# Table phases of a state-space convolution: made by TensorE from fp16 parts instead of by VectorE

## The chip, the cores and the metric

The kernel runs on one core of one Trainium2 chip. The metric is the device time of one execution in microseconds (us); a ratio is the time after over the time before. The engines are called PE (TensorE, matrix products into PSUM), DVE (VectorE), ACT (ScalarE), POOL (GpSimd) and SP (SyncE, which issues most DMAs).

## What is computed

A residual block over 2048 positions and 512 channels: a long convolution whose kernel is a sum over 128 complex exponentials, and then a channel MLP.

```python
dt = exp(log_dt)[:, None]                       # (512, 1)
P  = exp(dt*(A_re + 1j*A_im)[:, :, None] * l)   # l = 0..2047, rounded to bf16
K  = einsum("dn,dnl,dn->dl", C, P, dt*B).real   # (512, 2048), a sum over n = 128
y  = irfft(rfft(pad(u)) * rfft(pad(K)))[:L] + u*Dskip
h  = x + y                       # u = layernorm(x)
out = h + W2.gelu(W1.layernorm(layernorm(h)) + b1) + b2
```

The step that the change is about is K. Position l is split as l = 8k + rest, so that each exponential is a product of two small tables: a B table over k (33 entries, -16 to 16, of which entry 0 is one) and an A table over the other part (20 entries, the list LA). Every entry is 128 rows (n) by 512 channels, complex: exp(real part) times cosine and sine of a phase. The phase of a B entry is 8k*psi, that of an A entry LA*psi plus the angle gamma of C*B*dt; psi is dt*A_im in units of 1/65536 of a turn, so that the low 16 bits of an integer are the phase and wrap by themselves.

## The kernel before

**Order.** Every operation is added to a list with a priority, a cost and what it reads and writes. A list scheduler (class Sched) then sets one fixed order per engine before the kernel runs: it takes what can start first by its costs, and by priority where several can. PSUM is handed out by the same planner as four slots of 128x1024 f32 (ps0 to ps3). On the chip each engine works through its list in order and waits where something isn't ready. SBUF is one tile, `ar`, cut up by address, so most rows of the profile read `ar<-ar` or `ar<-ps`.

**Stages, in the order of the program.**
- Constants: DFT tables T, TP1, TP2, BD, DD, W from integer codes on DVE and sines on ACT (lines 400 to 575; L441 is the helper for ACT activations, L422, L424, L429 and L434 are helpers for DVE operations).
- Parameters: six inputs are transposed by PE (L587), and `th` = dt*A_re, `psi` = dt*A_im, the size G of the coefficient C*B*dt and its angle `gam` are made, all 128x512 f32.
- Exponentials: 32 ACT instructions for the B table (L597) and 20 for the A table (L600), each 128x512 from `th` with a scale. Ten DVE products (L786) multiply the A table by G.
- Layernorm statistics of x (L673), normalised u (L693, L695), block DFT by PE (L697), its results copied out of PSUM (L358 on ACT, L360 on DVE) and sent to DRAM and back (AU_d); then the transform of x (xspec, L715).
- Tables, in two halves of 256 channels (`tables(0)`, `tables(1)`). Each half has nine groups of four entries: four B groups and five A groups. For a group DVE makes 4 code pieces of 128x256 (L422 or L434) and a second copy a quarter turn on (L422, 128x1024); ACT takes Sin of the low 16 bits of all 2048 codes in one instruction (L441); DVE multiplies the exponentials by sine and cosine (L773, L774 and a sign change L772 for a B group, which makes entries k and -k; L787, L788 for an A group). Code buffers and sine buffers are three deep. The imaginary tables of both halves lie in the same place, so `tables(1)` cannot write before kgen has read `tables(0)`.
- kgen(c), for channel blocks c = 0 to 3 of 128: 256 small matmuls (L807, L808) in four column tiles of PE; 0 and 1 need the first half, 2 and 3 the second.
- kspec(b,c), inverse(b,c): the kernel's transform and the inverse one (L846, L858, L882, L888), each with a trip through DRAM (AK_d, Z_d) to change layout; b = 0 and 1 are the two halves of the output positions.
- tail and mlp: residual, statistics (L968), the MLP (L1007, L1024), the output. tail(b) needs all four channel blocks of inverse(b).

SP's queue holds all DMAs of these trips, in one order; a DMA that waits holds up all behind it.

Of the kernel before, what the change touches and what calls it, by code (L numbers as in the profile page):

```python
# [14 lines left out]
i16 = mybir.dt.int16  # L15
P = 128
# [4 lines left out]
CW = 128  # L21
NCH = 4
# [75 lines left out]
SZ = {f32: 4, bf16: 2, i32: 4, i16: 2}  # L98
# [31 lines left out]
class Sched:  # L130
# [10 lines left out]
    def add(self, eng, cost, fn, r=(), w=(), new=(), lat=0.0, pr=None, byts=0):  # L141
# [4 lines left out]
        o.pr = self.pr if pr is None else pr  # L146
        deps = set()
# [23 lines left out]
    def run(self, nslots):  # L171
# [83 lines left out]
def kernel(ctx, tc, A_u, A_A_re, A_A_im, A_B_re, A_B_im, A_C_re, A_C_im, A_log_dt, A_Dskip,  # L255
# [43 lines left out]
    tiny = take(f32, 1)  # L299
# [100 lines left out]
    S.pr = 1  # L400
    table("trig_and_small")
# [45 lines left out]

    def ident_fn():
# [6 lines left out]
    POOL(0.3, lambda: gp.iota(i1.ap(), pattern=[[1, 32]], base=0, channel_multiplier=0), w=[i1])  # L455
    i4 = ct(i32, 16)
# [57 lines left out]
    valD = ct(f32, 2, 16)  # L514
    AC(valD, codD, ACT.Sin, scale=SINSC, oap=lambda: valD.ap().rearrange("p a b -> p (a b)"), iap=lambda: low16(codD), tbl=True)
# [31 lines left out]
    valW = ct(bf16, 4, 32)  # L547
    AC(valW, codW, ACT.Sin, scale=SINSC, oap=lambda: valW.ap().rearrange("p a b -> p (a b)"), iap=lambda: low16(codW), tbl=True)
    for v in range(7):
        for g in range(4):  # L550
            TS(W[v], valW, msk[4 * v + g:4 * v + g + 1], None, ALU.mult, n=128, mode=4, oap=lambda v=v, g=g: W[v].ap()[:, :, 32 * g:32 * g + 32])
    pm = take(f32, 1) if False else ct(f32, 1)
# [3 lines left out]

    for f0 in range(0, 16, 4):
        for half, TPx in ((0, TP1), (1, TP2)):
            p = Ps()

            def fn(e, f0=f0, half=half, p=p):
                o = pst(p)
                idp = identb.ap().rearrange("p (a s r) -> p s a r", a=4, r=2)
                for k in range(4):
                    for r in range(2):
                        pe.matmul(o[64 * r:64 * r + 64, 128 * k:128 * k + 128], lhsT=T.ap()[:, f0 + k, half, :], rhs=idp, start=True, stop=True, tile_position=(0, 64 * r))  # L566
            add("PE", 0.9, fn, r=[T, identb], w=[p], new=[p], pr=3)
            oap = lambda f0=f0, TPx=TPx: TPx[f0:f0 + 4].ap().rearrange("p a b -> p (a b)")
            if half == 0:
                add("ACT", c_act(512, 1), lambda e, p=p, oap=oap: act.activation(oap(), pst(p)[:, 0:512], ACT.Copy, scale=pm.ap()), r=[p, pm], w=[TPx[f0:f0 + 4]], pr=3)  # L570
            else:
                evac(oap, lambda p=p: pst(p)[:, 0:512], 512, [p], [TPx[f0:f0 + 4]], pr=3)

    S.pr = 2
# [21 lines left out]
    for a in range(NA):  # L599
# [507 lines left out]
```

## Time and profile before

| | us |
|---|---|
| runs of the kernel (3) | 374.4, 375.73, 375.84; median 375.73 |
| span of the profiled execution, from its first to its last instruction | 373.3 |
| DVE busy in the span | 217.9 |
| PE busy in the span | 207.6 |
| ACT busy in the span | 195.5 |

The page gives no other time for the profiled execution than its span; the runs lie 1.1 to 2.5 us above it, and the median 2.4. The granted clock of PE is told from 103 us on; before that the page shows 1.00 for want of a record, and the pace of the matmuls tells the level. Read first which engine is full in which stretch (the 40 slices), then how each stage ends.

### The profile page before, as it was taken

To read this page: it belongs to the slowest core of one execution; us is meant where nothing else is said; L and a number is where in the kernel's file an instruction comes from. 1 tells how busy PE (TensorE), PEld (TensorE's weight loads), DVE (VectorE), ACT (ScalarE), POOL (GpSimd) and SP (SyncE) were. 2 spreads that over 40 slices of the span, in tenths; PEclk is the share of its full clock that TensorE was granted. 3 is DMA by queue.
4 is the path that set the end of the run, shared out by engine and by line. 5 is a ranking of instruction groups with operands and counts; after the bars stand their busy time and mean duration, and the time that the engine had idled before them with its cause. 6 is when DMAs were issued, how large, how long until landed. Compare 5 with 4: busy or idle time off the path is not lost.

```text
span 373.3 us, 6724 instructions
## 1 busy us (share of the span) xinstructions
PE 207.6 (56%) x2697; PEld 130.3 (35%) x2712; DVE 217.9 (58%) x524; ACT 195.5 (52%) x240; POOL 6.6 (2%) x72
## 2 busy tenths in 40 slices
PE   1012206637004632154654773669959998699994
PEld 1001102116004521154433672126737652344441
DVE  8999999969999399900113650495443604920202
ACT  1259899998448263820523475447624553473340
POOL 5000000000000000000000000000000000000000
PEclk9999999999656965558855595769978999989999
DMA  7300000899900223793667796400796531010101
GB/s 204 122 0 0 1 0 15 213 207 235 218 14 3 71 68 112 152 217 98 191 145 211 213 276 153 105 1 2 209 256 146 150 87 28 3 29 14 44 15 42
DMA packets 70946, 39.84 MB, mean 107 GB/s; under 512 B 56097, under 2 KB 65794, under 8 KB 70914
## 3 DMA queue, kind: packets, MB, share of 16 engines
q1 hardware_dynamic: 69186, 38.88, 41.5%
q10 hardware_dynamic: 1728, 0.52, 0.8%
q8 instruction: 21, 0.34, 0.4%
q14 instruction: 11, 0.09, 0.1%
HBM read 20.52 MB, written 14.68 MB: 94 GB/s over the span
## 4 chain that ended last, share of the span: by engine, by line
PE 36%; DVE 30%; DMA 15%; ACT 7%; issue 7%; SPq 3%; DVEq 0%; ACTq 0%
PE ps L1007 10%; PE ps L1024 9%; DMA ar<-AU_d 5%; DVE ar L434 4%; DMA AK_d<-ar 4%; DMA Z_d<-ar 4%; DVE ar L429 4%; ACT ar L358 3%; DVE ar L422 3%; SPq L370 3%; PE ps L888 3%; PE ps L807 3%; DVE ar L673 3%; PE ps L697 3%; PE ps L808 3%
## 5 line engine op out<-in xcount | busy, mean ns | idle before, releaser
L358 ACT CAST ar<-ps 128x1024 bf16<-128x1024 f32 (+2 forms) x86 | 73.7, 898 | 88.1 <-PE ps L808 22.9
L441 ACT ACTIVATE ar<-ar 128x2048 bf16<-128x2048 int16 (+5 forms) x30 | 41.9, 1415 | 38.4 <-DVE ar L422 18.6
L1007 PE MATMUL ps<-ar 128*128 128x512 bf16 (+1 forms) x170 | 42.8, 401 | 1.7 <-ACT ar L358 1.3
L876 DVE TENSOR_TENSOR ar<-ar 128x1024 bf16<-128x1024 bf16 x48 | 30.2, 685 | 22.2 <-PE ps L888 15.7
L1024 PE MATMUL ps<-ar 128*128 128x512 bf16 (+1 forms) x169 | 41.4, 390 | 1.4 <-DVE ar L1026 0.8
L1009 ACT ACTIVATE ar<-ps,ar 128x512 bf16<-128x512 f32 (+1 forms) x44 | 30.2, 688 | 22.0 <-PE ps L1007 12.8
L360 DVE CAST ar<-ps 128x1024 bf16<-128x1024 f32 (+1 forms) x22 | 24.2, 1121 | 28.7 <-DMA AK_d<-ar 16.2
L1026 DVE TENSOR_TENSOR ar<-ps,ar 128x512 bf16<-128x512 f32 x16 | 10.9, 688 | 46.4 <-PE ps L1024 35.9
L807 PE MATMUL ps<-ar 128*20 128x33 bf16 x512 | 18.9, 250 | 30.8 <-DVE ar L788 24.0
L807 PEld LDWEIGHTS <-ar 128*20 128x20 bf16 x512 | 17.4, 124 | 40.4 <-DVE ar L788 26.0
L422 DVE TENSOR_SCALAR ar<-ar 128x256 int32<-128x256 f32 (+8 forms) x103 | 28.8, 327 | 0.9
L1007 PEld LDWEIGHTS <-ar 128*128 128x128 bf16 (+1 forms) x176 | 18.3, 105 | 22.7 <-issue 5.8
L1024 PEld LDWEIGHTS <-ar 128*128 128x128 bf16 (+1 forms) x176 | 17.2, 100 | 20.4 <-issue 2.6
L808 PE MATMUL ps<-ar 128*20 128x33 bf16 x512 | 18.9, 249 | 9.0 <-issue 9.0
L715 PE MATMUL ps<-ar 128*128 128x128 bf16 x128 | 13.5, 285 | 18.2 <-DMA ar<-AU_d 11.5
L434 DVE SCALAR_TENSOR_TENSOR ar<-ar 128x256 int32<-128x256 f32 (+4 forms) x77 | 22.2, 321 | 1.6 <-ACT ar L441 0.5
L858 PE MATMUL ps<-ar 128*128 128x128 bf16 x128 | 11.4, 254 | 20.6 <-DMA ar<-AK_d 12.7
L846 PE MATMUL ps<-ar 20*128 20x256 bf16 (+1 forms) x448 | 18.3, 321 | 6.6 <-ACT ar L358 6.5
L968 DVE BATCH_NORM_STATS2 ar<-ps 128x6 f32<-128x512 f32 x16 | 10.4, 688 | 19.3 <-PE ps L963 14.8
L566 PE MATMUL ps<-ar 128*64 128x128 bf16 x64 | 5.0, 291 | 27.8 <-ACT ar L570 13.1
L715 PEld LDWEIGHTS <-ar 128*128 128x128 bf16 x128 | 11.5, 132 | 21.2 <-DMA ar<-AU_d 13.6
L597 ACT ACTIVATE ar<-ar 128x512 bf16<-128x512 f32 x32 | 16.7, 613 | 3.5 <-DVE ar L429 3.5
(65 smaller groups left out, 292.9 us busy)
## 6 DMA issues: line engine op xcount, KB each, us to landing
AU_d<-ar SPq DMA_DIRECT2D x16, 256.0 KB, 3.8
ar<-AU_d SPq DMA_DIRECT2D x8, 512.0 KB, 6.0
ar<-ar SPq DMA_DIRECT2D x16, 256.0 KB, 5.0
AK_d<-ar SPq DMA_DIRECT2D x16, 256.0 KB, 3.9
ar<-AK_d SPq DMA_DIRECT2D x8, 512.0 KB, 3.7
Z_d<-ar SPq DMA_DIRECT2D x16, 256.0 KB, 5.0
ar<-Z_d SPq DMA_DIRECT2D x8, 512.0 KB, 5.3
ar<-in_A_u_dram SPq DMA_DIRECT2D x6, 512.0 KB, 6.7
```

What stands on the lines that cost most here:

```text
L358: act.copy(out_fn(), in_fn())
L360: dve.tensor_copy(out_fn(), in_fn())
L422: dve.tensor_scalar(a, b, f(s1), None, op0)
L434: add("DVE", c_dve(n, 1, psum), lambda e: dve.scalar_tensor_tensor(oap() if oap else o.ap(), aap() if aap else a.ap(), f(s), bap() if bap ...
L441: add("ACT", c_act(n, len(r) - 1 - int(tbl)), lambda e: act.activation(oap() if oap else o.ap(), iap() if iap else i.ap(), func, bias=f(bi ...
L715: pe.matmul(pst(p)[:, 128 * k:128 * k + 128], lhsT=T.ap()[:, f0 + k].rearrange("p a b -> p (a b)"), rhs=X.ap()[:, f0 + k, :], start=True, ...
L807: pe.matmul(o, lhsT=Ar.ap()[:, :, d], rhs=Br.ap()[:, :, d], start=True, stop=False, tile_position=(0, 32 * g))
L808: pe.matmul(o, lhsT=Ai.ap()[:, :, d], rhs=Bi.ap()[:, :, d], start=False, stop=True, tile_position=(0, 32 * g))
L876: add("DVE", c_dve(1024, 2) + 0.1, lambda e, kf=kf, x=x, pr_=pr_, f0=f0: dve.tensor_tensor(pr_.ap(), kf[f0:f0 + 8].ap(), x[f0:f0 + 8].ap() ...
L1007: pe.matmul(pst(p)[:fs, 512 * z:512 * z + 512], lhsT=w1s[dc].ap()[:, fc * P:fc * P + fs], rhs=ybuf.ap()[:, dc, :], start=(dc == 0), stop=( ...
L1009: add("ACT", c_act(512, 1), lambda e, p=p, z=z, fc=fc, fs=fs: act.activation(hT.ap()[:fs, fc, :], pst(p)[:fs, 512 * z:512 * z + 512], ACT. ...
L1024: pe.matmul(pst(p)[:, 512 * z:512 * z + 512], lhsT=hT.ap()[:fs, fc, 128 * t:128 * t + 128], rhs=w2s[fc].ap()[:fs], start=(fc == 0), stop=( ...
```

## The change

Codes are no longer made by DVE. PE makes the phases (and the exponents of the A table) as matmuls, straight into PSUM, and ACT reads them there:

- `psi*8`, `psi`, `psi*256` and `gam` are wrapped to one turn, and each (with `th` and ln of the squared coefficient) is cut into an fp16 high part and an fp16 remainder (`split`, 128x512 each). Through DRAM they are laid out as rows 32q..32q+31 of four operands SB, SA, SG, ST.
- A stationary operand `LWT` of 74 blocks of 128x32 holds the multipliers (k, LA and so on) on a diagonal; a row of it adds 12582912 (or that plus a quarter turn) to the phase, so that the low half of the f32 word in PSUM is the phase as a 16-bit integer. ACT takes Sin of every other int16 of a PSUM slot.
- A group's sines become two ACT instructions of 1024 elements each. A slot for B takes 16 matmuls of 256 columns in four column tiles, one for A 32 (two for each result: LA*psi, and gamma with the constant). The A exponentials are made the same way: 10 slots of 8 matmuls of 512 columns, with the coefficient's size inside the exponent, so the ten products by G are gone.
- All exponentials come before any sine: the table set for exponentials is loaded first, and the constants' sines (T, BD, DD, W) move behind the last exponential. One of four table loads goes.
- The transposes of T (TP) get a low priority; the PE costs of the planner are lowered (0.9 to 0.55 or 0.52, 5.5 to 3.2, 0.036 to 0.026), its DMA rate too (220 to 190); a PSUM slot is kept free for the operation that comes first in the program among those that still want one.

```diff
-        while av:
+        wants = [o.i for o in ops if o.new]
...
-                if need > len(fs):
+                if need > len(fs) or (need and i != wants[0] and len(fs) - need < len(ops[wants[0]].new)):
...
+    def split(v, tile, q, nm):
+        hl = at(spl[0], f16, 2, 512)
...
+        add("DVE", c_dve(512, 2), lambda e: dve.tensor_copy(hl[0].ap(), v.ap()), r=[v], w=[hl[0]])
+        TT(hl[1], v, hl[0], ALU.subtract)
+        dd = dram.tile([P, 2, 512], f16, name=f"S_{nm}{q}")
+        dma("SP", lambda: dd[:], lambda: hl.ap(), 262144, [hl], [("D" + nm, q)])
+        for z in range(2):
+            dma("SP", lambda z=z: tile.ap()[32 * (q + z):32 * (q + z) + 32], lambda z=z: dd.rearrange("(j i) z d -> z i j d", j=4)[z], 131072, [("D" + nm, q)], [(nm, q + z)])
...
-    for a in range(NA):
-        add("ACT", c_act(512), lambda e, a=a: act.activation(multi(E0 + (NB + a) * 256, ESZ, bf16, NCH, CW), th.ap().rearrange("p (c d) -> p c d", c=NCH), ACT.Exp, scale=float(LA[a])),
...
+    for a in range(0, NA, 2):
...
+                    pe.matmul(pst(p)[32 * j:32 * j + 32, 512 * z:512 * z + 512], lhsT=LAE[a + z].ap(), rhs=ST.ap()[:, j, :], start=True, stop=True, tile_position=(0, 32 * j))
...
+    S.pr = 3
+    table("trig_and_small")
+    at_ = gi
+    AC(at_, gi, ACT.Arctan, tbl=True, pr=2.9)
...
+        def sines(sc, slot_of):
+            for kp in range(2):
+                p = Ps()
...
+                add("ACT", c_act(1024), lambda e, p=p, kp=kp: act.activation(sc.ap()[:, :, 2 * kp:2 * kp + 2, :], pst(p).bitcast(i16).rearrange("p (s k d two) -> p s k d two", s=2, k=2, two=2)[:, :, :, :, 0], ACT.Sin, scale=SINSC),
...
-            for j in range(4):
-                STT(cod[0][j], psi, -float(LA[a0 + j]), gam, ALU.mult, ALU.subtract, n=256, aap=lambda: csl(psi), bap=lambda: csl(gam))
-            TS(cod[1], cod[0], 16384.0, None, ALU.add)
...
+                    for s in range(2):
+                        for z in range(2):
+                            a = a0 + 2 * kp + z
+                            for j in range(4):
...
+                                    pe.matmul(o, lhsT=LA1[a].ap(), rhs=SA.ap()[:, j, ch0:ch0 + 256], start=True, stop=False, tile_position=(0, 32 * j))
+                                pe.matmul(o, lhsT=LG[s].ap(), rhs=SG.ap()[:, j, ch0:ch0 + 256], start=(a == 0), stop=True, tile_position=(0, 32 * j))
...
-            add("DVE", c_dve(1024, 2), lambda e, lo=lo: dve.tensor_tensor(ent(e0, lo, 4), ent(e0, lo, 4), Gv(), ALU.mult), r=rE + [G], w=rE, pr=pr - 0.5)
...
-        add("PE", 5.5 if b == 0 else 5.0, fn, r=[Kg[c], W], w=ps, new=ps)
+        add("PE", 3.2, fn, r=[Kg[c], W], w=ps, new=ps)
```

Where the planner puts things shows at three places. ACT from the constants' last sine to the first copy of a TP tile, before (L441 with 512 is a parameter step, L597 and L600 are B and A exponentials):

```order
L441 ACTIVATE ar<-ar 128x128
L352 ACT_TABLE_LOAD
L441 ACTIVATE ar<-ar 128x512
L597 ACTIVATE ar<-ar 128x4x128 x32
L441 ACTIVATE ar<-ar 128x512 x2
L600 ACTIVATE ar<-ar 128x4x128 x2
```

ACT from its first table load on, with the change (L446 is the helper that was L441, L608 B exponentials, L673 A exponentials from PSUM):

```order
L359 ACT_TABLE_LOAD
L446 ACTIVATE ar<-ar 128x512
L608 ACTIVATE ar<-ar 128x4x128 x13
L446 ACTIVATE ar<-ar 128x512 x2
L608 ACTIVATE ar<-ar 128x4x128 x19
L446 ACTIVATE ar<-ar 128x512 x4
L673 ACTIVATE ar<-ps_66 128x2x4x128
```

The exponentials now stand first on ACT, with the steps for the coefficient between them, and the constants' sines stand behind the tenth L673.

ACT when the block DFT (L697, copied out by L358) begins, before; L570 copies TP tiles, L695 normalises:

```order
L570 ACTIVATE ar<-ps_67,ar 128x512
L695 ACTIVATE ar<-ar 64x512
L358 CAST ar<-ps_66 128x1024
L358 CAST ar<-ps_67 128x1024
L695 ACTIVATE ar<-ar 64x512 x3
```

ACT at the same place with the change; L829 are table sines read from PSUM, L365 and L768 are the former L358 and L695:

```order
L446 ACTIVATE ar<-ar 128x128
L829 ACTIVATE ar<-ps_67 128x2x512
L829 ACTIVATE ar<-ps_65 128x2x512
L829 ACTIVATE ar<-ps_66 128x2x512
L829 ACTIVATE ar<-ps_67 128x2x512
L365 CAST ar<-ps_66 128x1024
L365 CAST ar<-ps_67 128x1024
L365 CAST ar<-ps_66 128x1024
L768 ACTIVATE ar<-ar 64x512 x4
L829 ACTIVATE ar<-ps_65 128x2x512
```

Sines of the first table groups now stand ahead of and between the copies of the block DFT, and share the PSUM slots with it; the TP tile in ps0 (64) is copied out only after ten of these copies.

DVE at the A groups of the first half, before:

```order
L422 TENSOR_SCALAR ar<-ar 128x1024
L434 SCALAR_TENSOR_TENSOR ar<-ar 128x256 x4
L422 TENSOR_SCALAR ar<-ar 128x1024
L787 TENSOR_TENSOR ar<-ar 128x2x512
L788 TENSOR_TENSOR ar<-ar 128x2x512
L434 SCALAR_TENSOR_TENSOR ar<-ar 128x256 x2
```

DVE at the same groups with the change (L367 is the former L360, copies for xspec; L874 and L875 the former L787 and L788):

```order
L367 CAST ar<-ps_65 128x1024
L367 CAST ar<-ps_67 128x1024
L874 TENSOR_TENSOR ar<-ar 128x2x512
L367 CAST ar<-ps_64 128x1024
L875 TENSOR_TENSOR ar<-ar 128x2x512
```

Only the products are left of an A group on DVE; copies for the transform of x, which stood ahead of the tables' last B group, now stand between them.

## Rows read from the trace of the kernel before

**Rows 1.** Page: busy tenths in 40 equal slices of 9.33 us, DVE.

```profile
DVE  8999999969999399900113650495443604920202
```

**Rows 2.** Busy time by stage: stretch, length, each engine's busy time (instructions), clock, DMA.

```profile
5.00:58.00 53.00, 7.99 (x80) 5.57 (x81) 51.34 (x174) 35.34 (x65) 1.08 (x21) 1.00 0.16 48
58.00:78.70 20.70, 14.34 (x40) 4.38 (x39) 18.70 (x30) 18.77 (x24) 0.63 (x2) 1.00 0.57 138
78.70:116.30 37.60, 7.25 (x65) 6.29 (x65) 34.75 (x70) 24.26 (x16) 0.00 (x0) 0.72 0.65 148
116.30:130.30 14.00, 9.61 (x512) 8.97 (x513) 8.29 (x24) 6.13 (x6) 0.00 (x0) 0.87 0.17 49
130.30:158.10 27.80, 7.57 (x146) 6.26 (x144) 26.86 (x50) 16.98 (x13) 0.00 (x0) 0.56 0.43 108
...
177.50:234.00 56.50, 33.17 (x562) 27.17 (x561) 16.99 (x21) 25.71 (x27) 0.52 (x1) 0.65 0.75 200
234.00:373.30 139.30, 118.17 (x784) 62.62 (x799) 56.72 (x153) 63.36 (x87) 0.00 (x0) 0.92 0.29 74
```

**Rows 3.** Timeline, 6 to 58 us: start, length, engine, line, operation, count, [wait before].

```profile
6.01 0.61 PE L587 MATMUL ps<-ar 128*128 128x128 bf16 x4 [6.01 <-DMA ar<-in_A_A_re_dram]
25.28 16.74 ACT L597 ACTIVATE ar<-ar 128x512 bf16<-128x512 f32 x32 [3.49 <-DVE ar L429]
49.61 8.41 ACT L600 ACTIVATE ar<-ar 128x512 bf16<-128x512 f32 x16
```

**Rows 4.** Groups by line and shape, DVE: count | busy us, mean ns | idle before.

```profile
L434 DVE SCALAR_TENSOR_TENSOR ar<-ar 128x256 int32<-128x256 f32 x40 | 14.5, 420 | 0.0
L422 DVE TENSOR_SCALAR ar<-ar 128x1024 int32<-128x1024 int32 x18 | 12.6, 697 | 0.6
L422 DVE TENSOR_SCALAR ar<-ar 128x256 int32<-128x256 f32 x32 | 7.6, 286 | 0.0
L786 DVE TENSOR_TENSOR ar<-ar 128x1024 bf16<-128x1024 bf16 x10 | 6.3, 682 | 0.0
```

**Rows 5.** The same view: DVE rows nearest to the added operations.

```profile
L429 DVE TENSOR_TENSOR ar<-ar 128x512 f32<-128x512 f32 x6 | 4.0, 682 | 0.0
L424 DVE TENSOR_SCALAR ar<-ar 128x512 f32<-128x512 f32 x3 | 1.3, 427 | 0.1
L429 DVE TENSOR_TENSOR ar<-ar 128x928 f32<-128x928 f32 x1 | 1.1, 1106 | 0.0
```

**Rows 6.** The same view, ACT.

```profile
L358 ACT CAST ar<-ps 128x1024 bf16<-128x1024 f32 x62 | 60.5, 1015 | 49.4 <-DMA AK_d<-ar 9.6 <-PE ps L888 7.9 <-PE ps L715 7.1
L441 ACT ACTIVATE ar<-ar 128x2048 bf16<-128x2048 int16 x19 | 36.1, 1922 | 24.9 <-DVE ar L422 18.6 <-DVE ar L774 3.5 <-DVE ar L424 1.6
L600 ACT ACTIVATE ar<-ar 128x512 bf16<-128x512 f32 x20 | 10.7, 613 | 0.0
```

**Rows 7.** Page: DMA issues of the inverse's trip: count, KB each, median us to landing.

```profile
Z_d<-ar SPq DMA_DIRECT2D x16, 256.0 KB, 5.0
ar<-Z_d SPq DMA_DIRECT2D x8, 512.0 KB, 5.3
```

**Rows 8.** Timeline of PE: block DFT, start of kgen, kspec; what ended a wait in brackets.

```profile
59.22 4.44 PE L697 MATMUL ps<-ar 64*128 64x512 bf16 x10
...
116.30 0.26 PE L807 MATMUL ps<-ar 128*20 128x33 bf16 x1 [24.01 <-DVE ar L788]
...
116.47 0.30 PE L808 MATMUL ps<-ar 128*20 128x33 bf16 x4
116.53 0.31 PE L807 MATMUL ps<-ar 128*20 128x33 bf16 x4
...
130.30 3.81 PE L846 MATMUL ps<-ar 20*128 20x256 bf16 x112
```

**Rows 9.** Timeline of PE: the last inverse product, MLP work, the second tail.

```profile
298.24 1.95 PE L888 MATMUL ps<-ar 128*128 128x128 bf16 x32
...
309.97 0.38 PE L958 MATMUL ps<-ar 128*128 128x512 bf16 x1
```

More of the change, by code (lines that the diff above doesn't have):

```diff
@@ L146, in add @@
         o.pr = self.pr if pr is None else pr
+        o.start = None
         deps = set()
@@ L194, in ready @@
             return t
+        wants = [o.i for o in ops if o.new]
         while av:
+            while wants and ops[wants[0]].start is not None:
+                wants.pop(0)
             fs = sorted((slots[s], s) for s in range(nslots) if taken[s] is None)
@@ L298 @@
     b1_sb = take(f32, 11)
-    tiny = take(f32, 1)
+    tiny = take(f32, 2)
     st = take(f32, 16, 6)
@@ L313 @@
     gam = take(f32, 512)
-    G = take(bf16, 512)
+    pos[0] += 1024
     cod0 = pos[0]
-    COD = [take(i32, 2, 4, 256) for _ in range(3)]
+    SB, SG, SA, ST = (take(f16, 4, 512) for _ in range(4))
+    LWT = take(f16, 74, 32)
+    pos[0] = cod0 + 24576
     sc0 = pos[0]
@@ L546 @@
     TS(codW, codW, 1024.0, 16384.0, ALU.mult, ALU.add, n=64, oap=lambda: codW.ap()[:, :, 0, :], iap=lambda: codW.ap()[:, :, 0, :])
[L547 to L552, printed above, removed]
+    pm = tiny[1:2]
     hp = bits(pi, 6, 1)
     TS(pm, hp, -2.0, 1.0, ALU.mult, ALU.add)
[L557 to L577, printed above, removed]
+    S.pr = 0
     table("natural_log_exp_and_others")
@@ L642 @@
     TS(sg, m, -2.0, 1.0, ALU.mult, ALU.add)
+    S.pr = 0.5
+    split(th, ST, 0, "ST")
+    split(s1, ST, 2, "ST")
+    S.pr = 0.6
+    p, pa = tr("aim")
+    STT(psi, p, 65536.0 / (2 * math.pi), dtb, ALU.mult, ALU.mult, psum=True, aap=pa)
+    q = ttmp(f32, 512)
+    wrap(psi, 1.0, q)
+    TT(psi, psi, q, ALU.add)
+    w8 = ttmp(f32, 512)
+    wrap(psi, 8.0, q)
+    STT(w8, psi, 8.0, q, ALU.mult, ALU.add)
+    split(w8, SB, 0, "SB")
+    S.pr = 0.7
+    split(psi, SA, 0, "SA")
+    wrap(psi, 256.0, q)
@@ new lines @@
+    S.pr = 3
+    table("trig_and_small")
+    at_ = gi
+    AC(at_, gi, ACT.Arctan, tbl=True, pr=2.9)
+    S.pr = 2.9
+    STT(at_, at_, 65536.0 / math.pi, sg, ALU.mult, ALU.mult)
+    STT(gam, m, 32768.0, at_, ALU.mult, ALU.add)
+    STT(gam, psi, 128.0, gam, ALU.mult, ALU.add)
+    wrap(gam, 1.0, q)
+    TT(gam, gam, q, ALU.add)
+    split(gam, SG, 0, "SG")
+    S.pr = 3
+    AC(T, codT, ACT.Sin, scale=SINSC, oap=lambda: T.ap().rearrange("p a b c -> p (a b c)"), iap=lambda: low16(codT), tbl=True)
@@ new lines, with fn @@
+    valW = ct(bf16, 4, 32)
+    AC(valW, codW, ACT.Sin, scale=SINSC, oap=lambda: valW.ap().rearrange("p a b -> p (a b)"), iap=lambda: low16(codW), tbl=True)
+    for v in range(7):
+        for g in range(4):
+            TS(W[v], valW, msk[4 * v + g:4 * v + g + 1], None, ALU.mult, n=128, mode=4, oap=lambda v=v, g=g: W[v].ap()[:, :, 32 * g:32 * g + 32])
+    for f0 in range(0, 16, 4):
+        for half, TPx in ((0, TP1), (1, TP2)):
+            p = Ps()
+            def fn(e, f0=f0, half=half, p=p):
+                o = pst(p)
+                idp = identb.ap().rearrange("p (a s r) -> p s a r", a=4, r=2)
+                for k in range(4):
+                    for r in range(2):
+                        pe.matmul(o[64 * r:64 * r + 64, 128 * k:128 * k + 128], lhsT=T.ap()[:, f0 + k, half, :], rhs=idp, start=True, stop=True, tile_position=(0, 64 * r))
+            add("PE", 0.9, fn, r=[T, identb], w=[p], new=[p], pr=12)
+            oap = lambda f0=f0, TPx=TPx: TPx[f0:f0 + 4].ap().rearrange("p a b -> p (a b)")
+            if half == 0:
+                add("ACT", c_act(512, 1), lambda e, p=p, oap=oap: act.activation(oap(), pst(p)[:, 0:512], ACT.Copy, scale=pm.ap()), r=[p, pm], w=[TPx[f0:f0 + 4]], pr=12)
+            else:
+                evac(oap, lambda p=p: pst(p)[:, 0:512], 512, [p], [TPx[f0:f0 + 4]], pr=12)
@@ L808, in fn @@
                             pe.matmul(o, lhsT=Ai.ap()[:, :, d], rhs=Bi.ap()[:, :, d], start=False, stop=True, tile_position=(0, 32 * g))
[L809 removed]
+            add("PE", 0.026 * 8 * sum(n for _, n in grp), fn, r=[Ar, Br, Ai, Bi], w=[p], new=[p])
             i0, n = grp[0]
```

163 lines of the change are left out of this document (97 added, 66 removed).

## The prediction, made before the changed kernel ran

> **What bounds the kernel now.** I read the 40 slices first: VectorE (DVE) is full for the first 17 of them, up to about 159 us, except for one dip at 121 to 130 us [rows 1]. The same in numbers, from the busy time by stage: DVE is busy 51.3 of 53.0 us, then 18.7 of 20.7, 34.8 of 37.6 and, after the dip, 26.9 of 27.8 [rows 2]. Then the timeline of PE at the first kgen, to see whether that full engine is what is waited for: its first matmul starts at 116.30, after PE waited 24.0 us for DVE's last A product [rows 8]. So to 116.3 each microsecond off DVE counts, as long as nobody else becomes late. In the dip (116.3 to 130.3) PE runs kgen 0 and 1 and DVE, busy 8.3 of 14.0, has no more to do until they have read the imaginary tables. Up to 158.1 DVE bounds again (second half of the tables). From 177.5 to 234 no engine is full (PE 33.2 of 56.5), and DMA moves 200 GB/s: this is the kernel's and the inverse's trips through DRAM. The last 139.3 us are PE, busy 118.2 [rows 2].
>
> **What goes.** From DVE: 40 code instructions of 0.36 us (14.5), 18 shifts by a quarter turn (12.6), 32 codes for B (7.6) and 10 products by G (6.3), 41.0 us in all [rows 4]. The G products and half of the codes belong to the first half of the tables and so lie ahead of 116.3: 6.3 + 34.7/2 = 23.7. From ACT 19 large sines less one that is a constant's (18 x 1.92 = 34.6) and 20 A exponentials (10.7) [rows 6], and one table load.
>
> **What comes, on DVE.** Five splits, each a cast and a subtraction of 128x512: the cast is bounded by a product and by a one-operand instruction of that size, 0.43 to 0.68; I take 0.43, since it has one operand, and 0.68 for the subtraction: 5.5. Three more wraps of two instructions, 6 x 0.43 = 2.6. Four more parameter steps for psi*8 and gam, 4 x 0.68 = 2.7. The product that makes the stationary operand, 2368 columns, scaled from 928 columns in 1.11: 2.8 [rows 5]. Sum 13.6, all ahead of 116.3. Net on DVE there: 13.6 - 23.7 = -10.
>
> **What comes, on ACT.** 36 sines of 1024 elements from PSUM. The nearest row is the copy of 1024 from PSUM, 1.015: 36.5; ten A exponentials alike, 10.2 [rows 6]. Together 46.7 against 45.3: +1.4, and it may be less if ACT isn't slowed by PSUM. ACT was busy 35 of 53 and 24 of 38 us there [rows 2], so the amount fits; the order is what matters. The exponentials start when `th` is ready: before, at 25.28, though the transposes of A_re were over at 6.6 [rows 3], since ACT and DVE made constants first. Now about 10: 32 of them take 16.7, so to 28; then the coefficient's logarithm and its split, an estimate of 35 on DVE; a trip through DRAM (two transfers, each bounded above by 5.3, the price of a larger one [rows 7]) brings the operand by 39 to 46, I take 44; ten A exponentials take 10, so they end at 54, where they ended at 58.0 before [rows 3]. But gamma's arctangent needs the other table set and so stands behind all of them: gam, its wrap and its split (some 4 us of DVE) come at 56 to 60, and DVE has less left to fill the wait with. I take 4 us of DVE waiting.
>
> **What comes, on PE.** The block DFT shows 0.444 us for 512 columns (4.44/10), so 0.222 for 256; kspec shows 112 matmuls of 256 columns in 3.81, 0.034 each, four tiles at a time, so 0.136 for a step of four [rows 8]. B slots: 16 of four steps; A slots: 20 of eight; 224 steps, 30 to 50 us; the exponentials' 10 slots have two steps of 0.444, 9. PE was busy 8.0 + 14.3 + 7.3 + 9.6 + 7.6 of 153 us up to 158 [rows 2]; an A slot at 1.1 to 1.8 us is at most 0.8 longer than the ACT instruction that reads it, and A groups have a DVE partner of 1.4. I price this at nothing, hidden by ACT and DVE; if the cover goes it is 5 slots x 0.8 = 4 us a half.
>
> At one place a rule speaks against this. The trace shows that the program's alternation L807, L808 is not kept: four L808 start, then four L807, in turn [rows 8]; it looks as if each column tile had its own queue, so two matmuls per tile need not halve the overlap. The Trainium skill, page "TensorE: Matmul & The Clock Gate", section "Part 3: Packing small matmuls — row/col tiling", says that matmuls keep program order in start and end, with no reordering. By that the pair of an A result, written one behind the other to the same tile, would let only two tiles overlap, and the sum would grow as in the last rival; by the row it doesn't, and I go by the row.
>
> **What moves.** Sines now stand ahead of and between the copies of the block DFT on ACT, in strict order, and share the PSUM slots with them, with one of four slots held by a TP tile. The block DFT stage took 20.7 us with PE 14.3, ACT 18.8 busy [rows 2]; six sines more are 6.1, which I let lengthen it (to about 84.5). Of the -10 on DVE, 4 are lost to the arctangent; the 6 of sines in the stage are work taken out of the next stage, where ACT was busy 24.3 of 37.6, and I count 1 of them as lost.
>
> **The sum,** against the span of the profiled execution, 373.3:
> - first kgen: -10 + 4 + 1 = -5, so at 111.5 (ends: -13, if DVE stays full and fills half of its former 6.5 us of idle time; +8, rival below);
> - kgen 0 and 1: 14.0 stays; PSUM is now one slot in turn for them: 0 (to +2);
> - second half: half of the codes is 17.4 us; 8.3 of it were hidden in the dip, and some 2 made before; 7 lay after 130.3. -7 (ends -9, and -2 if the 18 sines, 18.3 us, bound it);
> - kspec 0 and 1 and the transform of x now stand ahead of kgen 2 on PE: +1 (0 to 3);
> - 177.5 to 234: the first half's trip is through before the second half's kgen ends, so SP's queue and DMA have less in this stretch: -4 (0 to -10);
> - the end: between the last inverse product (ending 300.2) and the second tail (309.97) stood 9.8 us of MLP work [rows 9], which covers the trip through DRAM, 5.0 + 5.3 [rows 7]; now 25 matmuls of L1111 stand there, 5.5 if 512 columns take half of the block DFT's 0.444 [rows 8], since the granted clock is 0.92 there [rows 2] and the block DFT's pace is the lower level of 1.2 GHz: 4.3 uncovered, and I let 1.3 of it overlap the trip's first pieces: +3 (0 to +5).
>
> Sum -12: a span of 361.3. The runs of before lie 1.1 to 2.5 above the span, the median 2.4: **363.7**. With the ends, 352 to 372.
>
> **Rivals.**
> *More gain.* DVE stays full and nothing couples: kgen 0 at 103 (-13), second half -9, the DMA stretch -8, the end 0, others +1: 373.3 - 29 = 344, with half of it missing 354. For: ACT has idle time in each stage [rows 2]. Against: the arctangent, and three engines in strict order that must hand over 46 PSUM slots more.
> *No change.* The stretch to 234 is bound by transfers: at 200 GB/s, 75% of the DMA engines busy [rows 2], it gives back what the tables gain (-12 and +12, so 373 to 377), because SP's queue is one order and a transfer that waits holds up the rest. Against: the bytes are the same and start earlier.
> *Slower.* The hand-over on ACT: a sine that waits for a sine buffer (freed by DVE) has the copies of the block DFT behind it, these hold PSUM, and PE, then the trip of the transform, then DVE wait. If each of the 14 sine slots of that stage costs a wait of 1.4 (the DVE pair of an A group), kgen 0 comes at about 130 (+14); the other terms give -7: 380 + 2.4 = 382. It decides from kgen 0 later than 123.3, where +7 eats the -7. Against: ACT had 1.9 + 13.3 us of idle time after 58.
> *Pairs in order.* As said, 16 steps instead of 8 for 20 A slots: 160 x 0.222 = 35.5 more on PE, half ahead of kgen 0: about 398.
>
> **How the numbers follow.** Forecast (352 to 372) 0.62; more gain 0.14; no change 0.09; slower by the hand-over 0.12, by pairs in order 0.03. What a measurement can tell from no change is 0.5%, 373.8 to 377.6: faster 0.76, same 0.09, slower 0.15. For 8 in 10 I take 349 to 379: outside are half of more gain, half of the hand-over and the pairs, 0.16.
>
> **What would show it.** In the changed kernel's profile: exponentials (L608) start at about 10 and A exponentials (L673) end at 54; the sines (L829) take 1.0 each; an A slot takes PE 1.1 to 1.8 us, not 3.5; the first kgen (L894) starts at 111 and the third near 147; the first tail (L1045) starts at 220 to 225, against 234; before the second tail PE stands still for some 3 us. The forecast is wrong if kgen 0 starts after 123 (the hand-over), if kgen gains and the first tail doesn't (no change), or if DVE waits in A groups for sines that wait for PE.

## The result, and the profile after

The changed kernel took 354.22 us (median of 5 runs, 353.80 to 358.67) against 375.68 before: ratio 0.948, 95% interval 0.942 to 0.953. Two later groups of runs on other occasions gave 357.4 against 375.0 (0.953, 0.948 to 0.957) and 357.6 against 374.7 (0.954, 0.949 to 0.959). The forecast was 363.7, in a range of 349 to 379; it had the sign and 56% of the gain of the first group (12.0 of 21.5 us), 69% of that of the later ones. Single executions of the changed kernel lie mostly near 355 or near 359 us, and the first profile (span 356.9) is of the longest of its group, 358.67, so it shows 16.4 of the 21.5 us. A second profile, taken later (after_third), has a span of 353.3.

The page of the changed kernel, 40 slices of 8.92 us, PE, DVE, ACT and what DMA moved; [rows 1] has DVE before:

```profile
PE   1200084779796549866952764499999977599994
DVE  7899997989990059740702541873655323941102
ACT  2792299887795137822734451565648312362430
GB/s 166 173 68 168 59 2 35 133 175 164 232 234 157 72 73 61 155 206 169 200 248 247 249 252 59 2 0 113 176 237 180 100 103 41 1 0 17 44 15 44
```

The same kernel by stage, cut where its stages begin; the columns are those of [rows 2] (stretch, length, PE, weight loads, DVE, ACT, POOL, clock, DMA share, GB/s):

```profile
5.00:58.00 53.00, 12.35 (x152) 6.39 (x152) 47.44 (x131) 34.05 (x52) 11.95 (x102) 0.98 0.33 101
58.00:78.70 20.70, 15.02 (x102) 5.96 (x102) 19.35 (x61) 18.31 (x25) 0.42 (x1) 0.50 0.51 128
78.70:111.70 33.00, 28.61 (x608) 21.20 (x604) 26.54 (x39) 29.00 (x33) 0.20 (x1) 0.84 0.91 208
111.70:128.80 17.10, 10.06 (x512) 9.07 (x513) 0.18 (x1) 1.96 (x3) 0.00 (x0) 0.85 0.28 71
128.80:148.80 20.00, 15.61 (x398) 12.93 (x396) 18.90 (x32) 15.19 (x17) 0.00 (x0) 0.79 0.35 98
148.80:167.00 18.20, 11.28 (x529) 10.16 (x530) 4.98 (x7) 4.72 (x6) 0.00 (x0) 0.75 0.89 198
167.00:219.00 52.00, 30.40 (x588) 26.76 (x587) 18.31 (x22) 23.48 (x25) 0.52 (x1) 0.73 0.87 222
219.00:356.90 137.90, 117.98 (x785) 62.01 (x799) 60.92 (x158) 58.19 (x82) 0.00 (x0) 0.92 0.27 69
```

Read it from the ends. DVE is no longer full ahead of kgen 0: it is busy 26.5 of the last 33.0 us, where it had 34.8 of 37.6; PE (28.6) and ACT (29.0) are now the busiest there. During kgen 0 and 1 it has 0.18 us of work where it had 8.3, since no codes are left to make ahead. The second half's stretch is 20.0 us instead of 28.6, and the last 137.9 us are PE's as before.

What the planner's order did to the start of kgen 0 is seen in DVE's timeline (start, length, count, wait before) ...

```profile
105.80 0.69 DVE L875 TENSOR_TENSOR ar<-ar 128x1024 bf16<-128x1024 bf16 x1
121.09 0.18 DVE L907 TENSOR_TENSOR ar<-ar 128x32 bf16<-128x32 bf16 x1 [14.59 <-ACT ar L365]
128.90 0.69 DVE L853 TENSOR_TENSOR ar<-ar 128x1024 bf16<-128x1024 bf16 x1 [7.63 <-PE ps L895]
```

... beside that of PE (L867 and L868 are phases of A groups, L843 of B groups):

```profile
100.99 0.30 PE L867 MATMUL ps<-ar 128*32 128x256 f16 x4
...
104.72 2.04 PE L843 MATMUL ps<-ar 128*32 128x256 f16 x64
107.07 0.62 PE L843 MATMUL ps<-ar 128*32 128x256 f16 x16 [0.31 <-ACT ar L829]
107.99 0.62 PE L843 MATMUL ps<-ar 128*32 128x256 f16 x16 [0.30 <-ACT ar L829]
108.91 0.62 PE L843 MATMUL ps<-ar 128*32 128x256 f16 x16 [0.30 <-ACT ar L829]
109.82 0.62 PE L843 MATMUL ps<-ar 128*32 128x256 f16 x16 [0.30 <-ACT ar L829]
110.74 0.29 PE L868 MATMUL ps<-ar 128*32 128x256 f16 x4 [0.30 <-ACT ar L829]
```

DVE ends the first half's products at 106.5; before, kgen 0 waited for just that [rows 8]. Now it waits behind phases of the *second* half, which stand ahead of it on PE and go at the pace at which ACT's sines free PSUM, until 111.75. By the lines above these are nine slots: eight of B (16 matmuls of L843 each) and one of A.

### The profile page after: what moved, and what is told of

The parts are those of the page before. It is cut to its first block, busy times and chain, and to the rows that moved or that the text cites. A ratio compares the mean times of both kernels' runs of the same rounds, so it can differ in the third digit from the quotient of the medians.

```text
span 356.9 us, 8713 instructions
## 1 busy us (share of the span) xinstructions
PE 241.3 (68%) x3658; PEld 154.5 (43%) x3672; DVE 200.1 (56%) x451; ACT 186.2 (52%) x241; POOL 16.7 (5%) x158
## 4 chain that ended last, share of the span: by engine, by line
PE 47%; DVE 19%; ACT 12%; DMA 11%; issue 7%; SPq 2%; ACTq 0%; DVEq 0%
PE ps L1094 12%; PE ps L1111 10%; ACT ar L365 5%; DVE ar L434 4%; PE ps L975 4%; PE ps L969 3%; PE ps L895 3%; ACT ar L829 3%; PE ps L894 3%; DMA ar<-in_A_B_im_dram 3%; ACT ar L673 3%; DMA ar<-Z_d 2%; SPq L377 2%; PE ps L933 2%; DVE ar L439 2%
## 5 line engine op out<-in xcount | busy, mean ns | idle before, releaser
L365 ACT CAST ar<-ps 128x1024 bf16<-128x1024 f32 (+3 forms) x84 | 71.2, 888 | 92.6 <-PE ps L895 28.3
L367 DVE CAST ar<-ps 128x1024 bf16<-128x1024 f32 (+1 forms) x24 | 28.1, 1177 | 32.7 <-PE ps L945 18.1
L1111 PE MATMUL ps<-ar 128*128 128x512 bf16 (+1 forms) x170 | 39.8, 379 | 2.0 <-DVE ar L1113 1.7
L829 ACT ACTIVATE ar<-ps 128x1024 bf16<-128x1024 int16 x36 | 34.6, 1037 | 7.2 <-DVE ar L854 6.5
L895 PE MATMUL ps<-ar 128*20 128x33 bf16 x512 | 19.8, 249 | 11.6 <-issue 11.6
L671 PE MATMUL ps<-ar 128*32 128x512 f16 x80 | 7.0, 511 | 29.9 <-DMA ar<-S_ST 29.6
L1111 PEld LDWEIGHTS <-ar 128*128 128x128 bf16 (+1 forms) x176 | 16.9, 98 | 20.8 <-issue 2.2
L895 PEld LDWEIGHTS <-ar 128*20 128x20 bf16 x512 | 17.9, 125 | 15.5 <-issue 15.5
L894 PE MATMUL ps<-ar 128*20 128x33 bf16 x512 | 19.5, 250 | 3.3 <-ACT ar L365 2.3
L868 PE MATMUL ps<-ar 128*32 128x256 f16 x320 | 21.5, 308 | 0.3 <-ACT ar L829 0.3
L867 PE MATMUL ps<-ar 128*32 128x256 f16 x304 | 20.9, 308 | 0.6 <-ACT ar L365 0.6
L434 DVE TENSOR_TENSOR ar<-ar 128x4 f32<-128x4 f32 (+5 forms) x60 | 19.9, 335 | 1.3
L1055 DVE BATCH_NORM_STATS2 ar<-ps 128x6 f32<-128x512 f32 x16 | 10.5, 690 | 17.9 <-PE ps L1050 13.3
L608 ACT ACTIVATE ar<-ar 128x512 bf16<-128x512 f32 x32 | 16.8, 613 | 3.8 <-DVE ar L434 3.8
L894 PEld LDWEIGHTS <-ar 128*20 128x20 bf16 x512 | 17.4, 124 | 1.7 <-DVE ar L875 1.1
L1050 PE MATMUL ps<-ar 128*64 128x512 bf16 x48 | 10.0, 470 | 11.6 <-DMA ar<-Z_d 10.9
L671 PEld LDWEIGHTS <-ar 128*32 128x32 f16 x80 | 2.9, 124 | 33.8 <-issue 33.3
```

What stands on the lines that cost most here:

```text
L365: act.copy(out_fn(), in_fn())
L367: dve.tensor_copy(out_fn(), in_fn())
L434: add("DVE", c_dve(n, mode, psum), lambda e: dve.tensor_tensor(oap() if oap else o.ap(), aap() if aap else a.ap(), bap() if bap else b.ap( ...
L829: add("ACT", c_act(1024), lambda e, p=p, kp=kp: act.activation(sc.ap()[:, :, 2 * kp:2 * kp + 2, :], pst(p).bitcast(i16).rearrange("p (s k ...
L867: pe.matmul(o, lhsT=LA1[a].ap(), rhs=SA.ap()[:, j, ch0:ch0 + 256], start=True, stop=False, tile_position=(0, 32 * j))
L868: pe.matmul(o, lhsT=LG[s].ap(), rhs=SG.ap()[:, j, ch0:ch0 + 256], start=(a == 0), stop=True, tile_position=(0, 32 * j))
```

## Experiments

Each is the changed kernel, or the one before, with one edit. "kgen 0" is the start of the first kgen, "second half" the time from the end of the second kgen to the start of the third.

**The changed kernel twice more.**

> The changed kernel once more, for a second profile: its first profiled execution had a span of 356.9 us where four further executions had 352.0 to 352.8. If the 4 us are the clock (0.850 there, 0.863 to 0.868 in the others), the stages up to the first tail keep their places (first kgen at 111.7, third at 148.8, first tail at 219.0) within 2 us and the difference lies where PE is full, after 219. If they are one long wait, one of these places moves by the whole 4 us.

> The changed kernel again, as the reference of this group of runs (its time was 354.2 against 375.7 before, and 357.4 against 375.0 in the second group). Expected 354 to 358; the first kgen at 112, the third at 149, the first tail at 219.

Measured: 357.4 (355.3 to 359.2) and 357.6 (355.1 to 359.3). The profile of after_again (span 357.4) has its stages within 1 us of the first one's: kgen 0 at 112.5, the third kgen at 149.2, the first tail at 219.5. That of after_third (353.3) differs. Between the first profile and after_third the difference builds up in steps: 1.6 us by kgen 0, 3.1 by the end of the fourth kgen, 5.3 by the first tail, and 1.7 is lost again after it. So it is neither only the clock at the end nor one wait, as the expectation had offered; its cause stays open, and an edit of 3 us can't be judged from one execution.

**The planner alone, in the kernel before.**

```diff
+        wants = [o.i for o in ops if o.new]
...
-                if need > len(fs):
+                if need > len(fs) or (need and i != wants[0] and len(fs) - need < len(ops[wants[0]].new)):
...
-                dma_busy = b + o.byts / 220e3
+                dma_busy = b + o.byts / 190e3
...
-        add("PE", 5.5 if b == 0 else 5.0, fn, r=[Kg[c], W], w=ps, new=ps)
+        add("PE", 3.2, fn, r=[Kg[c], W], w=ps, new=ps)
...
```

> The kernel before with the planner of the changed one and nothing else: its PE costs, its DMA rate of 190, the PSUM slot kept free. My theory: the gain is VectorE's, 41 us of codes and products taken away, so the first kgen stays at 116 and the third at 159 and the time at 376, within 3 us. Rival: the gain after 177 us comes from the order that the lowered costs make; then the stretch from the fourth kgen's end to the first tail shortens from 56.5 to about 52, and the time is 371 or less.

Measured: 371.5, ratio 0.989 (0.984 to 0.994), so the rival was right, if barely (it named 371 or less): some 3 us come from the order alone. kgen 0 is at 114.15 and the third at 155.6, but the fourth kgen ends no earlier (177.9), and what is left of the gain is the stretch from there to the first tail, 52.8 instead of 56.5, as the rival had it. After that the second tail comes 2.2 us later and the end 1.4 us sooner than those stretches took before (78.4 and 61.7 us).

**The planner's numbers of before, in the changed kernel.** All of them (old_costs), then the DMA rate alone (rate_alone, the diff); the slot kept free stays.

```diff
-                dma_busy = b + o.byts / 190e3
+                dma_busy = b + o.byts / 220e3
```

> The changed kernel with the planner's PE costs and DMA rate of before (0.9, 5.5 and 5.0, 0.036; 220); the PSUM slot is still kept free. My theory: the first kgen starts at 112 and the third at 149 as in the changed kernel, and the time stays at 354 within 4 us. Rival: the order by costs brings 5 us or more, and the time is 359 to 365.

> The changed kernel with the planner's DMA rate of before alone (220 for 190); its PE costs stay low. old_costs gained 5.6 us against the changed kernel. If the rate does it, this gives 351 to 353; if it is the PE costs, which let MLP work go ahead of the transforms and leave PE without cover at the second tail, this stays at 355 to 358 and the last inverse still ends 67 us after the first tail starts, against 62 in old_costs.

Measured: 351.9 (ratio 0.938, 0.934 to 0.941) and 349.9 (0.935, 0.930 to 0.939), against 0.953 for the changed kernel in old_costs' group and 0.948 to 0.954 in all. Of old_costs' two theories the rival falls by sign, and mine holds only against the first group's 354: in its own group the old numbers are *better*, by 5.6 us. rate_alone, whose group has no run of the changed kernel, is better by 5 to 7 us by the ratios, so the rate is enough by itself. In rate_alone kgen 0 starts at 109.6 and the first tail at 212.0. Its end shows what a planned order is worth. PE from the last inverse product (L975) to the second tail (L1045, L1050; L1111 is MLP work), in the changed kernel ...

```profile
284.16 1.95 PE L975 MATMUL ps<-ar 128*128 128x128 bf16 x32
285.95 3.19 PE L1111 MATMUL ps<-ar 128*128 128x512 bf16 x13
289.98 2.54 PE L1111 MATMUL ps<-ar 128*128 128x512 bf16 x11 [0.84 <-DVE ar L1113]
292.35 0.38 PE L1045 MATMUL ps<-ar 128*128 128x512 bf16 x1
296.30 0.62 PE L1050 MATMUL ps<-ar 128*64 128x512 bf16 x4 [3.57 <-DMA ar<-Z_d]
```

... and in rate_alone:

```profile
273.81 1.95 PE L975 MATMUL ps<-ar 128*128 128x128 bf16 x32
275.60 6.43 PE L1111 MATMUL ps<-ar 128*128 128x512 bf16 x29
282.87 2.54 PE L1111 MATMUL ps<-ar 128*128 128x512 bf16 x11 [0.84 <-DVE ar L1113]
285.24 0.38 PE L1045 MATMUL ps<-ar 128*128 128x512 bf16 x1
285.55 0.63 PE L1050 MATMUL ps<-ar 128*64 128x512 bf16 x4
```

With 40 matmuls of L1111 left to do the trip through DRAM is covered; with 25 PE waits 3.6 us (one of the 25 has no record here; after_third shows 14 + 11 and a wait of 3.52). The rate of 190 is below what DMA moves here: the slices of the page show 247 to 252 GB/s from 178 to 214 us. How the rate makes this order was not followed through the planner.

**kgen first.** PE may make the second half's phases only between and after the parts of kgen 0 and 1.

```diff
-                add("PE", cost, fn, r=r + [TBL], w=[p], new=[p])
+                add("PE", cost, fn, r=r + [TBL] + ([('kg', min(ng, 4) - 1)] if hf else []), w=[p], new=[p])
...
-        for grp in KIS:
+        for gi_, grp in enumerate(KIS):
...
-            add("PE", 0.026 * 8 * sum(n for _, n in grp), fn, r=[Ar, Br, Ai, Bi], w=[p], new=[p])
+            add("PE", 0.026 * 8 * sum(n for _, n in grp), fn, r=[Ar, Br, Ai, Bi], w=[p] + ([('kg', 2 * c + gi_)] if c < 2 else []), new=[p])
```

> The changed kernel with one order edit: PE may make the second half's phases only between and after the parts of kgen 0 and 1, two slots after each part, where seven slots stood ahead of kgen 0. In the changed kernel DVE ends the first half's products at 106.5 and kgen 0 starts at 111.75, behind seven slots that go at the pace of ACT's sines. If those slots are what kgen 0 waits for, it starts at 107, the second kgen ends at 123 to 125 instead of 128.8, DVE begins the second half as much earlier, and the time falls by 3 to 5 us, to 350. Rival: the second half is then late by as much, since its sines are the bound (18 of 1.03 us): the third kgen stays at 148 and the time at 354.

Measured: 351.0, ratio 0.933 (0.928 to 0.938), 6.4 us better than the changed kernel in the same group. kgen 0 starts at 104.95 and waits for DVE again:

```profile
104.95 0.27 PE L894 MATMUL ps<-ar 128*20 128x33 bf16 x4 [1.75 <-DVE ar L875]
```

The second kgen ends at 122.3, the third starts at 143.9. So the slots of the second half were what kgen 0 waited for (nine by the trace, the expectation counts seven), and the second half did not become late by as much (21.6 us instead of 20.0).

**DVE's old work put back** as idle work, PE still making the phases (`codes`, left out here, makes four 256-wide instructions, a shift, for A groups a product, all into scrap, and a group's sine waits for them by `tok`).

```diff
-                    r=[p, TBL], w=[sc])
+                    r=[p, TBL, tok], w=[sc])
...
-            sines(sc, slot_b)
+            sines(sc, slot_b, codes("B", ng))
...
```

> The changed kernel with VectorE's old work put back as idle work: for each group of four entries four code instructions of 128x256 and the shift by a quarter turn (as 768 and 256 elements), for an A group also a product of 128x1024, into a scrap buffer that nothing uses; by the planner a group's sine waits for it, three groups ahead at most, as the code buffers were. PE still makes the phases. Some 42 us in all, 24 of them ahead of kgen 0. My theory, that the gain is this work taken off DVE: kgen 0 starts at 125 to 131 (106.5, where DVE is done with the products now, plus 24, less up to 6 us of waits that it fills), the third kgen 6 to 7 us later than that adds, and the time is 372 to 382, at or above the kernel before. Rival: the gain comes from the order (exponentials first, the planner); then the time stays under 362.

> dve_back with a scrap buffer that no later load shares: in dve_back the buffer lay where rows of x are loaded for the last part, so DVE waited 4.7 us for that load in the middle of the second half and the output was overwritten. The work put back is the same 41 us (the shift as three instructions of 256 elements, the product as two of 512). kgen 0 should start at 125 to 131 again (129.8 in dve_back); the second half's stretch, from the second kgen's end to the third's start, 20 us in the changed kernel and 28.6 before, should be 27 to 31 without that wait (38.5 in dve_back); the time 376 to 384. Rival: the stretch stays near 38, so what lengthens it in dve_back is the order and not the wait, and the time is near 388.

Measured: 388.3 (1.038, 1.035 to 1.042) and, with the scrap buffer moved, 387.6 (1.031, 1.025 to 1.038), both slower than the kernel before and 30 us slower than the changed one. dve_back by stage, and its kgen 0:

```profile
58.00:78.70 20.70, 12.77 (x82) 4.58 (x82) 20.05 (x69) 14.93 (x20) 0.21 (x1) 0.50 0.29 77
78.70:129.80 51.10, 32.93 (x553) 23.69 (x552) 47.99 (x87) 32.17 (x38) 0.20 (x1) 0.70 0.65 145
...
146.70:185.20 38.50, 19.58 (x434) 15.58 (x431) 31.79 (x57) 18.83 (x20) 0.00 (x0) 0.72 0.46 106
```

```profile
129.79 0.28 PE L914 MATMUL ps<-ar 128*20 128x33 bf16 x4 [7.75 <-DVE ar L895]
```

kgen 0 waits for DVE again and starts where expected, at 129.8 in a DVE that is busy 48.0 of 51.1. So DVE's work is what the change buys: the whole change gains 17 to 21 us, some 3 of them by the planner's order, and with the work put back nothing of that is left, though everything else of the change is still in.

The sizes don't close as well. The total was put too low (372 to 382, then 376 to 384), and the idle work is dearer than what it stands for: DVE is busy 248.8 us in dve_back and 245.7 in dve_back2 against 200.1 in the changed kernel, so 48.7 and 45.6 us were put back where 41.0 had gone (four code instructions take 1.80 us where they took 1.42). Of the 13 us between dve_back2 and the kernel before, some 5 may be this; the rest would lie within the 13.6 worked out for the splits, wraps and LWT that come on DVE (no run took these alone). In dve_back's second half DVE is busy 31.8 us, against 26.9 before [rows 2], and waits 4.7 for the load, and that makes up nearly all of the 9.9 us by which the stretch is longer than before. I had blamed the load alone; moving the buffer did not bring the time down. Whether it brought the stretch to 27 to 31 us stays open.

**PE's part.** The first matmul of each A result twice (pe_more, the diff), or left out (pe_less).

```diff
+                                for _ in range(1 if a else 0):
+                                    pe.matmul(o, lhsT=LA1[a].ap(), rhs=SA.ap()[:, j, ch0:ch0 + 256], start=True, stop=True, tile_position=(0, 32 * j))
                                 if a:
                                     pe.matmul(o, lhsT=LA1[a].ap(), rhs=SA.ap()[:, j, ch0:ch0 + 256], start=True, stop=False, tile_position=(0, 32 * j))
```

> The changed kernel with the first matmul of each A result issued twice (16 more in a slot of 32, the result is the same). In the changed kernel three A slots take PE 2.8 us and three sines take ACT 2.9 to 3.1, so PE is just hidden. I expect 0.4 us more for each of 20 slots on PE, of which what lies above ACT's 1.03 shows: the time grows by 4 to 6 us, to 359 to 362, with kgen 0 near 114. Rival 1: PE is hidden with room, no change within 2 us. Rival 2: PE already sets the pace and clock is lost as well, 8 us or more, 364 and above.

> The changed kernel without the first matmul of each A result: the part of the phase in LA*psi is left out, so the A table holds gamma alone, and a slot has 16 matmuls instead of 32. If PE is hidden behind ACT's sines (1.03 a slot against 0.95 on PE), kgen 0 stays at 112 and the time within 2 us of the changed kernel. Rival: PE sets the pace of the A groups where its clock is low (a slot 1.8 us at half the clock), and the third kgen starts 2 to 4 us earlier than 149; the time falls by as much.

Measured: 360.2 for pe_more (0.966, 0.961 to 0.971; the changed kernel 0.953 and 0.954 in the groups before and after) and 357.1 for pe_less (0.952, 0.946 to 0.958; 0.954 in the same group). Taking half of an A slot away brings nothing, half as much again costs some 3 to 5 us: PE was hidden, and just so. In pe_more the cost is in the second half, 23.4 us instead of 20.0, so the third kgen starts at 152.0 where three profiles of the changed kernel have 146.7 to 149.2; kgen 0 does not move (112.3), though 114 was expected.

**The two orders together.** kgen first with the old costs and rate, and with the old rate alone.

> The edit of kgen_first and that of old_costs together. kgen_first brought 6.4 us (357.4 to 351.0), nearly all of it up to the first tail; old_costs 5.6 (357.4 to 351.9), 4.5 of it between the first and the second tail by the profile. They act in different stretches, so I expect 5 to 10 us together against the changed kernel: 346 to 350, with kgen 0 at 105 and 62 to 63 us between the last inverse and the first tail. Rival: the planner's order upsets one of the two, and the time is 351 or more.

> The edit of kgen_first with the planner's DMA rate of before (220), PE costs as changed. rate_alone gave 349.9 and first_and_old_costs 347.8. If the gains add where they act, kgen 0 starts at 105, the first tail at 206 to 211, and the time is 343 to 348. Rival: the gain of rate_alone ahead of the first tail (kgen 0 2 us, first tail 7 us earlier) is the same time that kgen_first takes, and the time is 349 or 350.

Measured: 347.8 (0.928, 0.925 to 0.931) and **344.96** (0.921, 0.918 to 0.925; 343.96 to 346.15). The second is the best version here: 12.6 us below the changed kernel in the same group. kgen 0 at 104.4, the first tail at 209.9, and before the second tail no wait for the trip.

## Why the prediction was right, and where not

The time lay in the range, and the mechanism forecast as the main one, work off VectorE ahead of kgen 0 and in the second half, is what the runs show. The sum hides errors that cancel in part, which is luck: kgen 0 and 1 lost 3 us that were not counted, the end gained where a loss was counted, and two terms had the right size for another reason.

The terms, with the two profiles of the changed kernel (before - first profile, and after_third), in us:

| term | forecast | first profile | after_third |
|---|---|---|---|
| kgen 0 starts (116.30; 111.75; 110.14) | -5 | -4.6 | -6.2 |
| kgen 0 and 1 (14.1; 17.1; 16.7) | 0 | +3.0 | +2.6 |
| second half, with kspec ahead of kgen 2 (28.6; 20.0; 19.9) | -7 + 1 | -8.6 | -8.7 |
| kgen 2 and 3 (18.6; 18.2; 17.2) | 0 | -0.4 | -1.4 |
| to the first tail's Z (56.5; 52.0; 49.8) | -4 | -4.5 | -6.6 |
| to the second tail's Z (76.2; 77.3; 78.0) | +3 | +1.1 | +1.8 |
| to the end (63.0; 60.6; 61.6) | 0 | -2.4 | -1.4 |
| sum | -12 | -16.4 | -20.0 |

**What goes and comes on DVE** was right as worked: net -10 ahead of kgen 0. DVE is busy 93.3 us from 5 us to the end of its last product, where it was busy 104.8 up to kgen 0 [rows 2], and that product ends at 106.5 instead of 116.2. Single prices were close: the cast 0.421, LWT's product 2.61 (2.8 forecast). One count was wrong, six splits instead of five, since the A exponents need two.

**What was lost of the -10** came out at the forecast size, 5, for another reason. I had put 4 to the arctangent; DVE waited 2.3 us for it:

```profile
56.48 2.15 DVE L439 SCALAR_TENSOR_TENSOR ar<-ar 128x512 f32<-128x512 f32 x3 [2.33 <-ACT ar L446]
```

The 5 us went to the order on PE, nine slots of the second half ahead of kgen 0, which I did not name. kgen_first shows it. This is a right number with a wrong reason.

**ACT** went as told. Groups by line and shape (count, busy, mean ns):

```profile
L829 ACT ACTIVATE ar<-ps 128x1024 bf16<-128x1024 int16 x36 | 34.6, 1037 | 7.2 <-DVE ar L854 6.5 <-PE ps L868 0.6
L608 ACT ACTIVATE ar<-ar 128x512 bf16<-128x512 f32 x32 | 16.8, 613 | 3.8 <-DVE ar L434 3.8
L673 ACT ACTIVATE ar<-ps 128x1024 bf16<-128x1024 f32 x10 | 9.3, 1067 | 6.3 <-PE ps L671 6.3
```

A sine costs 1.04 (the copy's 1.015 was the bound), B exponentials start at 10.4, the A exponentials end at 54.5, the block DFT ends at 84.6 (84.5 forecast). The slower rival, the hand-over on ACT, is there in small: sines waited 6.5 us for the buffers that DVE frees (L854), 2.5 of them ahead of kgen 0 and 4.1 in the second half; what kgen 0 waited for in the end was the order on PE.

**PE** was priced at nothing, and pe_less bears that out. The price named in case the cover went, 5 slots x 0.8 a half, counts too few: a half has ten A slots, so it would be 8 us.

**kgen 0 and 1** were put at 0 (to +2) and took 3 more. The one PSUM slot was named but not priced. Of the nine slots made ahead only six had been read by a sine, as many as the three sine buffers hold; the next sine ends its wait for a buffer at 132.19. So three PSUM slots stay full, all four parts go through the last one, and PE waits for ACT's copies 0.85 + 0.57 + 0.85 us, where no part waited for a copy before:

```profile
117.13 0.26 PE L895 MATMUL ps<-ar 128*20 128x33 bf16 x1 [2.90 <-issue]
118.99 0.28 PE L894 MATMUL ps<-ar 128*20 128x33 bf16 x4 [0.85 <-ACT ar L365]
121.11 0.27 PE L894 MATMUL ps<-ar 128*20 128x33 bf16 x4 [0.57 <-ACT ar L365]
125.41 0.25 PE L895 MATMUL ps<-ar 128*20 128x33 bf16 x1 [1.83 <-issue]
127.26 0.28 PE L894 MATMUL ps<-ar 128*20 128x33 bf16 x4 [0.85 <-ACT ar L365]
```

The gaps that the profile calls issue are not new: 4.4 us in three before, 4.7 in two now. They come mostly 128 matmuls and as many weight loads apart. Each of the twelve in the four kgens of both traces ends 1.3 to 1.6 us after a 16 KB transfer of the instruction queue (q8 on the page) has ended, so PE seems to wait there for its next instructions; no run tested it.

**The second half** measured -8.6 against -6, within the ends that were given. **To the first tail** the size was right (-4.5 and -6.6 against -4), the reason not. I had DMA move less in this stretch. It moved as much, 11.5 MB (52.0 us at 222 GB/s, 49.8 at 232 in after_third) where it was 11.3 (56.5 at 200 [rows 2]), in less time. planner_alone, with DVE's work all there, has 52.8 us at 199 GB/s, 10.5 MB, so most of this term can come from the order alone; what makes the rate higher with the change is open.

**The end** is the term that failed. The step itself came true: 25 matmuls of L1111 cover too little, and PE waits 3.57 us for the trip. But I priced it as a loss by itself. Before, PE waited for the transform's input (AU_d) in the same stretch. PE's waits (in all, times, longest) in the last part of the kernel before:

```profile
PE ps L715 <- DMA ar<-AU_d: 4.1, 2, 3.9
```

Now no such wait is in the list: the transform (L788) stands behind MLP work and starts without one. And what is done early is not left for later: the last part is 1.4 to 2.4 us shorter. Work that moves from one gap to another costs the difference of the gaps, and both terms together came to -1.3 and +0.4 instead of +3. planner_alone has the same matmuls ahead of its second tail (13 + 11 recorded), then a gap of 3.80 us, and +2.2 and -1.4 in the two stretches: this term goes with the planner's order, not with the codes.

**The rivals.** No change fell: the stretch that DMA fills moves 222 GB/s where it moved 200 and keeps its gain. Pairs in order fell. The trace shows 32 matmuls of an A slot starting in fours of one line, in turn, 0.11 us from four to four:

```profile
102.97 0.29 PE L867 MATMUL ps<-ar 128*32 128x256 f16 x4
103.08 0.29 PE L868 MATMUL ps<-ar 128*32 128x256 f16 x4
103.19 0.29 PE L867 MATMUL ps<-ar 128*32 128x256 f16 x4
103.30 0.29 PE L868 MATMUL ps<-ar 128*32 128x256 f16 x4
```

Eight such steps make 0.88 us a slot at the granted clock of 1.00 in this stretch, eight and not sixteen; at 86.5 to 89.4 us, where it is 0.50, a step takes 0.21 and a slot 1.7 (forecast 1.1 to 1.8). The rule of the Trainium skill that was weighed (page "TensorE: Matmul & The Clock Gate", section "Part 3: Packing small matmuls — row/col tiling": matmuls keep program order in start and end) would have given sixteen; the measurement decides, and pe_less shows that a slot of half the matmuls gains nothing. More gain did not come in the changed kernel, but first_and_rate shows that it was there: a span of 343.8 against the 344 that this rival named, once two orders are put right.

## What to carry to other kernels

When work leaves the bounding engine, ask which instruction is next in the *order* of the engine that waited: here PE's queue held nine slots of later work, and half of what DVE saved was spent behind them. A planner's numbers are part of a change: one of them, a DMA rate put below what DMA moves in the trips, cost 5 to 7 us of the gain, and only an experiment that undid it alone could tell. Price a new wait against the one that it replaces in the same stretch. And when work is put back as idle work, read what it took: here 46 to 49 us for 41.

## What the runs showed of the hardware

ACT reads every second int16 of PSUM words, 1024 of them, in 1.04 us, as fast as it copies 1024 f32 from there (1.018 in the changed kernel). PE at a granted clock of 1.00 takes 32 matmuls of 256 columns on four column tiles in 0.88 us even where two of a pair follow each other on one tile. In a long run of matmuls of 33 columns, each with its weight load, PE stood still for 1.1 to 4.1 us mostly once in 128 of them, and went on 1.3 to 1.6 us after a 16 KB transfer of the instruction queue had ended.
